# Moving background zero writes into a chain's idle stretches, and selecting row sums ahead of the last chunks

## Chip, cores, metric

One core of one Trainium2 chip. The metric is the device time of one execution in microseconds (us). A run is called slow when it lies more than 1.5% above the fastest run of the same kernel; medians below are of all runs, ratios and their 95% intervals of the fast runs alone.

## The reference

Two layers of attention and MLP for a single token, forward and backward: the output and the gradients of eight inputs.

```python
def _A_ref(x, k_cache, v_cache, wq, wo):          # D 1024, 32 heads of 128, 4 KV heads
    W = min(4096, max(256, Sk // 4))              # Sk 32768, so W = 4096
    q = (x @ wq) ...
    k = jnp.repeat(k_cache[:, :, Sk - W:, :], rep, axis=1)
    v = jnp.repeat(v_cache[:, :, Sk - W:, :], rep, axis=1)
    p = _softmax(einsum(q, k) * Dh ** -0.5)
    return einsum(p, v) ... @ wo
def _B_ref(x, w1, b1, w2):                        # D 1024, F 3584, Mish
    h = x @ w1 + b1
    return (h * jnp.tanh(softplus(h))) @ w2
x = x + _A_ref(_layernorm(x), ...)                # A1
x = x + _B_ref(_layernorm(x), ...)                # B2
x = x + _A_ref(_layernorm(x), ...)                # A3
x = x + _B_ref(_layernorm(x), ...)                # B4
_out, _vjp = jax.vjp(_f, A_x, A_k_cache, A_v_cache, A_wq, A_wo, B_w1, B_b1, B_w2)
```

Only the last 4096 of 32768 rows of the caches are used, so seven eighths of the gradients of both caches are zeros that have to be written: 58.7 MB, a third of all bytes that the kernel moves.

## The kernel before

The zeros are 112 transfers of 0.524 MB from one tile of zeros. A table says how many are issued at which point of the program; `zeros` puts them on the queue of the loads and outputs, `bg_zeros` on GpSimd's queue, behind a small copy that waits for a given tile. What the table leaves goes out at the end (the entry `W2` is read nowhere, so its two zeros do too).

```python
    def zeros(n):
        for _ in range(min(n, len(zero_jobs))):
            nc.sync.dma_start(zero_jobs.pop(0), zt[:])
    def bg_zeros(n, after):
        if n:
            nc.gpsimd.tensor_copy(gate_t[:], after[:, 0:1])
        for _ in range(min(n, len(zero_jobs))):
            nc.gpsimd.dma_start(zero_jobs.pop(0), zt[:])
    ...
    Z = dict(A3=16, B4=[0, 0, 0, 2, 0, 2, 6], A3c=6, A3d=18, W2=2, W1=3, A1c=2, A1d=20, end=8)
```

The chain runs: A1, B2, A3 forward; B4 forward and backward turned into one pass over w1 (below "the MLP", with `B4` the zeros ahead of each of its seven blocks); backward of A3; a second pass over w2; w1 backward; backward of A1; then **the tail**, which makes the weight and cache gradients and stores them. A matrix-vector product by rows streams the weights past the vector and leaves four partial rows in PSUM (the memory that TensorE writes to), from which `rows_sel2` copies and selects the sums as columns:

```python
    def rows_sel2(bank, out_of):
        yr = work.tile([P, 512], FP32, name="yr", tag="kp")
        nc.vector.tensor_copy(yr[:], bank[:])
        for j in range(4):
            mm(out_of(j), yr[:, j * P:(j + 1) * P], sel2[:], out_of.first and j == 0, True)
    ...
        for c in range(NW2):                      # w2_pass, 14 chunks
            w = pre.pop(0) if pre else w2_load(c)
            for tt in range(2):
                rows_y(yrow, w[:, tt, :], a_bf[:, 2 * c + tt:2 * c + tt + 1], tt, c == 0, c == NW2 - 1)
            ...                                   # transposes, ACT copy, DVE reduction, backward columns of c - 1
        bwd1(held.pop(), NW2 - 1)
        rows_sel2(yrow, Cols8(acc.cols(0, TD), False))
        nc.vector.tensor_add(x_new[:], x_col[:], acc.cols(0, TD))
```

Of the kernel before, what the change touches and what calls it, by code (L numbers as in the profile page):

```python
# [23 lines left out]
def kernel(  # L24
# [191 lines left out]
    def acc_tile(n):  # L216
        return pacc.tile([P, n], FP32, name="acc", tag="acc")

    def sm_tile(m, n):
        return pacc.tile([m, n], FP32, name="sm", tag="sm")  # L220
# [9 lines left out]
    def rows_y(bank, row, col, par, start, stop):  # L230

        for half in range(2):
            row_mm(bank, 2 * half + par, col, row[:, half * 512:half * 512 + 512], start, stop)

    def rows_sel2(bank, out_of):

        yr = work.tile([P, 512], FP32, name="yr", tag="kp")
        nc.vector.tensor_copy(yr[:], bank[:])
        for j in range(4):
            mm(out_of(j), yr[:, j * P:(j + 1) * P], sel2[:], out_of.first and j == 0, True)  # L240

# [171 lines left out]
    def attn_fwd(x_col, lname, first):  # L413
# [101 lines left out]
            nc.scalar.activation(p_bf[:, hf * 512:(hf + 1) * 512], hv[hf][:], ACT.Exp, bias=nm2[:, 0:1], scale=1.0)  # L515
        sv["p"] = p_bf
        yrow = acc_tile(512)
        late, early = list(range(NR, NO)), list(range(NR))
        order = early + late if first else late[0:1] + early + late[1:]
        for i, c in enumerate(order):  # L520
            if c not in held and c not in early:
                held[c] = wo_load(c)
            w = wo_kept[c] if c < NR else held.pop(c)
            for tt in range(2):
                rows_y(yrow, w[:, tt, :], o_bf[:, 2 * c + tt:2 * c + tt + 1], tt, i == 0, i == NO - 1)
            if not first and i == 0:
                held[NO - 1] = wo_load(NO - 1)
            if not first:
                if c < NR:
                    xq["wo"].extend(w[:, tt, :] for tt in range(2))  # L530
        yps = sm_tile(P, TD)
        rows_sel2(yrow, Cols8(yps, True))
        x_new = keep.tile([P, TD], FP32, name=f"x_{lname}")
        nc.vector.tensor_add(x_new[:], x_col[:], yps[:])
        return x_new, sv

    def mish_exp(h_ps, n):
# [32 lines left out]
            mm(big[:, t * P:(t + 1) * P], rep8[:, t, :], ident_bf[:], t % 4 == 0, True)  # L570
        return big

    def w2_pass(a_bf, g_bf, x_col, xname, wgname, gbc):

        acc = wide(TD + NW2)
        yrow = sm_tile(P, 512)
        wg = keep.tile([P, NW2, 2], FP32, name=wgname)
        held = []

        def bwd1(w, c):  # L580
            for dch in range(TD):
                mv(acc, TD + c, w[:, 1, dch * P:(dch + 1) * P], g_bf[:, dch:dch + 1], c == 0 and dch == 0, dch == TD - 1)

        for c in range(NW2):
            w = pre.pop(0) if pre else w2_load(c)
            for tt in range(2):
                rows_y(yrow, w[:, tt, :], a_bf[:, 2 * c + tt:2 * c + tt + 1], tt, c == 0, c == NW2 - 1)
            ps = psum1([P, 8, P], BF16, "tps")
            for b in range(TD):
                nc.tensor.transpose(ps[:, b, :], w[:, 1, b * P:(b + 1) * P], ident_bf[:])  # L590
            nc.scalar.copy(w[:, 1, :], ps[:].rearrange("p b c -> p (b c)"))  # L591
            scr = work.tile([P, D], BF16, name="scr", tag="kp")
            nc.vector.tensor_tensor_reduce(out=scr[:], in0=w[:, 0, :], in1=gbc[:], scale=1.0, scalar=0.0,  # L593
                                           op0=ALU.mult, op1=ALU.add, accum_out=wg[:, c, 0:1])
            if held:
                bwd1(held.pop(), c - 1)
            held.append(w)
        bwd1(held.pop(), NW2 - 1)
        rows_sel2(yrow, Cols8(acc.cols(0, TD), False))
        x_new = keep.tile([P, TD], FP32, name=xname)  # L600
        nc.vector.tensor_add(x_new[:], x_col[:], acc.cols(0, TD))
        nc.vector.tensor_copy(wg[:, :, 1:2], acc.cols(TD, TD + NW2)[:, :, None])
        return x_new, wg

    def mlp_fwd(x_col, lname, g_bf):

        n32, n_bf, rstd = ln_fwd(x_col, lname)
        sv = dict(n32=n32, rstd=rstd)
        hacc = wide(TF)
        h_init(hacc.t, 0, TF)  # L610
        for i in range(2 * TD):
            t, hf = i // 2, i % 2
            w = w1_load(i)
            for b in range(NW2):
                fb = hf * NW2 + b
                o = (b // 2) * 2 * P + b % 2
                mv(hacc, fb, w[:, o:o + 2 * P - 1:2], n_bf[:, t:t + 1], False, t == TD - 1)
        a_bf = pair_col("a", lname, TF)
        dact = keep.tile([P, TF], FP32, name=f"dact_{lname}")
        gbc = bcast_row(g_bf)  # L620
        m = mish_exp(hacc.cols(0, TF), TF)
        mish_w(m, hacc.cols(0, TF))
        nc.vector.tensor_mul(a_bf, m["hr"], m["w_"])
        mish_y(m)
        nc.vector.tensor_mul(dact[:], m["y"], m["r"])
        sv["dact"] = dact
        x_new, wg = w2_pass(a_bf, g_bf, x_col, f"x_{lname}", "wg4", gbc)
        return x_new, sv, wg

    CB = 512  # L630
# [8 lines left out]
    def mlp_turn(x_col, lname, wg, g_col, nxt):  # L639
# [28 lines left out]
                xpose(*alt_blocks(wf[:, k * 1024:(k + 1) * 1024], 4), None, True)  # L668

        for b in range(NBK):  # L670
            bg_zeros(Z["B4"][b], dh_bf[:, lo0(b):])
            ws[b] = [w1_block(b, hh) for hh in range(2)]
            lo = b * FB
            sl = slice(lo, lo + FB)
            hps = Wide(pacc.tile([P, FB * R16], FP32, name="sm", tag="sm"), FB)
            h_init(hps.t, lo, FB)
            for t in range(TD):
                for f in range(FB):
                    o = (f // 2) * 2 * P + f % 2
                    mv(hps, f, ws[b][t // HT][:, t % HT, o:o + 2 * P - 1:2], n_bf[:, t:t + 1], False, t == TD - 1)  # L680
            m = mish_exp(hps.cols(0, FB), FB)
            X(b, 0)
            mish_w(m, hps.cols(0, FB))
            q = work.tile([P, HQ], FP32, name="q_", tag="hr2")[:, 0:FB]
            nc.vector.tensor_mul(q, wgf[:, sl], m["r"])
            mish_y(m)
            nc.vector.tensor_mul(dh_bf[:, sl], m["y"], q)
            nc.vector.tensor_mul(dh[:, sl], m["y"], q)
            nc.vector.tensor_mul(a_bf[:, sl], m["hr"], m["w_"])
            ev[0] += 2.4  # L690
            ev[1] += 0.3
            if b:
                M(b - 1)
            X(b, 1)
            fill(4, ["wo", "V", "K", "wq"], None, True)
# [36 lines left out]
    def attn_bwd(g_col, g_bf, lname, sv, first, nxt):  # L732
# [112 lines left out]
            if not first and h % 8 == 7:  # L845
                run(1)
        nps = sm_tile(P, TD)
        rows_sel2(nrow, Cols8(nps, True))
        return ln_bwd(nps[:], sv["n32"], sv["rstd"], g_col, lname, nxt)


# [160 lines left out]
        slots.extend(strm.tile([P, 2048], BF16, name="st_o", tag="st")[:] for _ in range(NB))  # L1012
        dw_tall("w2", TF, out_8.rearrange("(c p t) d -> c p t d", p=P, t=2))

    Z = dict(A3=16, B4=[0, 0, 0, 2, 0, 2, 6], A3c=6, A3d=18, W2=2, W1=3, A1c=2, A1d=20, end=8)


    x1 = None
# [39 lines left out]
    x3, sA3 = attn_fwd(x2, "A3", False)  # L1058
    g3, g3b, sB4 = mlp_turn(x3, "B4", wg4, gcol, "A3")
    g2, g2b = attn_bwd(g3, g3b, "A3", sA3, True, "B2")  # L1060
    x4, wg2 = w2_pass(sB4["a_bf"], g2b, x3, "x_B4", "wg2", bcast_row(g2b))
    dh_of(wg2, "B2", sB2)
    x4_bf = keep.tile([P, TD], BF16, name="x4_bf")
    nc.vector.tensor_copy(x4_bf[:], x4[:])
# [81 lines left out]
```

## Time and profile before

| | before |
|---|---|
| time, median of 2 (range) | 489.98 us (488.81 to 491.14) |
| profiled span | 487.5 us |
| chain, to the start of the last step of A1's backward | 339.9 us |
| from there to the end | 147.6 us |
| zeros issued in the tail | 37 of 112 |

The slices and the table by stretch of this profile stand in the prediction. In the lines of a profile PE is TensorE (matmuls), PEld its weight loads, DVE VectorE, ACT ScalarE, POOL GpSimd and SPq the queue of SyncE; the granted clock is the share of full speed at which TensorE was let run, the DMA share the mean busy share of the 16 DMA engines.

The chain's end is read from the timeline of VectorE (DVE): the start of the instruction that writes the pair gX, the last that every kernel here has before the tail. Span less that time I call "the tail with its lead"; it needs no choice of window and serves to compare all kernels. The stretches of the chain are cut the same way, at the instructions that write x_A (twice), x_B (twice), gA_pair (twice) and gB_pair.

### The profile page before, as it was taken

How to read it: one execution, taken by the hardware profiler on the slowest of the kernel's cores; microseconds unless marked ns; L12 is line 12 of the kernel's file. 1: busy time of each engine (PE TensorE's matmuls, PEld its weight loads, DVE VectorE, ACT ScalarE, POOL GpSimd, SP SyncE). 2: the span in 40 equal slices, each digit the busy share in tenths (PEclk: the TensorE clock that was granted, in tenths of full speed). 3: DMA queues.
4: the chain of work that ended last, by engine and by line, in shares of the span. 5: the costliest groups of instructions: out<-in, count | busy, mean ns of one | idle time of the engine just before them, and what ended most of it. 6: DMA issues, size and time to landing. Idle time of an engine off the chain costs nothing.

```text
span 487.5 us, 11182 instructions
## 1 busy us (share of the span) xinstructions
PE 324.4 (67%) x4700; PEld 213.0 (44%) x4700; DVE 248.6 (51%) x521; ACT 219.5 (45%) x268; POOL 64.1 (13%) x160
## 2 busy tenths in 40 slices
PE   0676654777879998689788877776585873148200
PEld 0344223555549998569467875533311220011000
DVE  2224010573416776535486556455688994169500
ACT  1131100272426887758174536012398995059300
POOL 2000000002400124223001010200821222000000
PEclk9988555595988999998888899556655555555555
DMA  8999988997995799999469998994599999999997
GB/s 326 388 413 413 406 351 319 361 342 283 400 353 183 250 304 404 416 415 414 182 228 366 361 330 314 419 399 179 200 401 408 405 406 403 417 419 415 412 416 308
DMA packets 52253, 172.19 MB, mean 353 GB/s; under 512 B 5200, under 2 KB 12396, under 8 KB 51180
## 3 DMA queue, kind: packets, MB, share of 16 engines
q1 hardware_dynamic: 38816, 123.22, 65.7%
q0 software_dynamic: 13344, 48.25, 25.0%
q8 instruction: 37, 0.61, 0.5%
q14 instruction: 12, 0.10, 0.1%
q10 hardware_dynamic: 44, 0.01, 0.0%
HBM read 72.89 MB, written 98.58 MB: 352 GB/s over the span
## 4 chain that ended last, share of the span: by engine, by line
PE 18%; DMA 16%; issue 7%; DVE 6%; ACT 5%; SPq 1%; POOL 1%; DVEq 0%; ACTq 0%; POOLq 0%
DMA out_dram<-st_o 8%; PE tps L187 6%; DMA w_c<-in_B_w_dram 4%; PE acc L223 3%; DVE wq_b L146 3%; PE ops L223 3%; DMA wo_c<-in_A_wo_dram 2%; DMA out_dram<-so 2%; ACT wo_b L149 2%; PE sm L223 2%; PE d L223 1%; SPq L961 1%; PE tps L590 1%; ACT wo_c L149 1%; DVE st_o L146 1%
## 5 line engine op out<-in xcount | busy, mean ns | idle before, releaser
L139 POOL DMA_DIRECT2D out_dram<-zt x92 | 49.2, 538 | 79.6 <-DMA out_dram<-zt 78.5
L591 ACT COPY w_c<-tps 128x1024 bf16<-128x1024 bf16 x28 | 28.3, 1012 | 24.5 <-PE tps L590 13.8
L146 DVE CAST wo_b<-ops 128x512 bf16<-128x512 f32 (+3 forms) x40 | 33.2, 877 | 9.6 <-PE ops L223 8.1
L593 DVE CUSTOM_DVE_ANT_0 scr<-w_c,gbc 128x1024 bf16<-128x1024 bf16 x28 | 34.2, 1221 | 6.6 <-DMA w_c<-in_B_w_dram 4.5
L149 ACT CAST wo_b<-ops 128x512 bf16<-128x512 f32 (+2 forms) x34 | 27.2, 867 | 17.9 <-PE ops L223 16.5
L149 ACT COPY K<-tps 128x1024 bf16<-128x1024 bf16 x19 | 18.7, 1028 | 28.0 <-PE tps L187 27.9
L223 PEld LDWEIGHTS <-w_c 128*128 128x128 bf16 x672 | 22.9, 101 | 15.6 <-DMA w_c<-in_B_w_dram 10.1
L146 DVE CAST K<-ops 128x1024 bf16<-128x1024 f32 x15 | 17.7, 1222 | 16.0 <-DMA out_dram<-K 15.3
L149 ACT CAST K<-ops 128x1024 bf16<-128x1024 f32 x17 | 16.8, 1013 | 17.7 <-DMA out_dram<-K 15.8
L223 PE MATMUL q<-wq_b,nA_pair 128*32 128x512 bf16 x128 | 13.5, 520 | 16.3 <-DMA wq_b<-in_A_wq_dram 14.8
L149 ACT COPY w_b<-tps 128x1024 bf16<-128x1024 bf16 x20 | 19.5, 1015 | 4.6 <-PE tps L187 4.4
L146 DVE COPY K<-tps 128x1024 bf16<-128x1024 bf16 x13 | 8.8, 689 | 24.9 <-PE tps L187 24.9
L757 DVE CUSTOM_DVE_ANT_0 wo_c<-wo_c,gbc 128x1024 bf16<-128x1024 bf16 x14 | 16.4, 1219 | 9.7 <-DMA wo_c<-in_A_wo_dram 7.6
L187 PE MATMUL tps<-ident_bf,K 128*128 128x128 bf16 x256 | 21.0, 244 | 0.2 <-ACT K L149 0.2
L590 PE MATMUL tps<-ident_bf,w_c 128*128 128x128 bf16 x224 | 20.5, 245 | 0.0
L223 PE MATMUL ops<-Tw 2*128 2x512 bf16 x56 | 15.4, 545 | 5.9 <-ACT wo_b L149 4.1
L187 PEld LDWEIGHTS <-K 128*128 128x128 bf16 x256 | 17.8, 111 | 3.6 <-issue 3.5
L223 PE MATMUL ops<-Two 2*128 2x512 bf16 x64 | 12.5, 597 | 9.9 <-ACT wo_b L149 4.8
L146 DVE CAST st_o<-ops 128x512 bf16<-128x512 f32 (+3 forms) x20 | 16.3, 845 | 5.2 <-DMA out_dram<-st_o 3.7
L590 PEld LDWEIGHTS <-w_c 128*128 128x128 bf16 x224 | 15.1, 109 | 7.9 <-issue 7.9
L187 PE MATMUL tps<-ident_bf,w_c 128*128 128x128 bf16 x224 | 17.2, 237 | 1.9 <-DMA w_c<-in_B_w_dram 1.9
L149 ACT COPY w_c<-tps 128x768 bf16<-128x768 bf16 (+1 forms) x14 | 11.6, 830 | 14.0 <-PE tps L187 12.8
(334 smaller groups left out, 680.5 us busy)
## 6 DMA issues: line engine op xcount, KB each, us to landing
out_dram<-zt POOLq DMA_DIRECT2D x92, 512.0 KB, 12.0
wo_c<-in_A_wo_dram SPq DMA_DIRECT2D x28, 512.0 KB, 6.5
w_c<-in_B_w_dram SPq DMA_DIRECT2D x32, 448.0 KB, 6.0
w_c<-in_B_w_dram SPq DMA_DIRECT2D x28, 512.0 KB, 6.4
out_dram<-zt SPq DMA_DIRECT2D x20, 512.0 KB, 8.6
out_dram<-wo_b SPq DMA_DIRECT2D x18, 512.0 KB, 9.7
wq_b<-in_A_wq_dram SPq DMA_DIRECT2D x16, 512.0 KB, 11.6
out_dram<-K SPq DMA_DIRECT2D x8, 1024.0 KB, 24.5
```

The source lines that it names most:

```text
L139: nc.gpsimd.dma_start(zero_jobs.pop(0), zt[:])
L146: nc.vector.tensor_copy(out_ap, in_ap)
L149: nc.scalar.copy(out_ap, in_ap)
L187: nc.tensor.transpose(ps[:, b, :], ap, ident_bf[:])
L223: nc.tensor.matmul(out_ap, lhsT=lhsT, rhs=rhs, start=start, stop=stop, skip_group_check=True, **kw)
L590: nc.tensor.transpose(ps[:, b, :], w[:, 1, b * P:(b + 1) * P], ident_bf[:])
L591: nc.scalar.copy(w[:, 1, :], ps[:].rearrange("p b c -> p (b c)"))
L593: nc.vector.tensor_tensor_reduce(out=scr[:], in0=w[:, 0, :], in1=gbc[:], scale=1.0, scalar=0.0, op0=ALU.mult, op1=ALU.add, accum_out=wg[:, ...
L757: nc.vector.tensor_tensor_reduce(out=w[:, 0, :], in0=w[:, 0, :], in1=gbc[:], scale=1.0, scalar=0.0, op0=ALU.mult, op1=ALU.add, accum_out=w ...
L961: nc.sync.dma_start(out_v[c], st[:])
```

## The change

Part 1 moves zeros out of the tail into stretches where the DMA row had dips. Part 2 ends the row products early: all but the last two or three chunks go as rows, their sums are copied and selected while the last chunks are awaited, and the last chunks go as column products straight into the same PSUM columns. In the W2 passes VectorE's reduction now writes over the weights in place of a scratch tile, and (not in the cut) the five zeros of the MLP's first block wait for the layer norm's output. The diff cut to its core (the two attentions differ in where the selection stands):

```diff
-    Z = dict(A3=16, B4=[0, 0, 0, 2, 0, 2, 6], A3c=6, A3d=18, W2=2, W1=3, A1c=2, A1d=20, end=8)
+    Z = dict(B2=2, A3=16, B4=[5, 1, 1, 2, 1, 2, 6], A3c=6, A3d=26, W1=3, A1c=4, A1d=28, end=4)
 # attention
+        NRW = NO - 2 if first else NO - 3
-            for tt in range(2):
-                rows_y(yrow, ..., i == 0, i == NO - 1)
+            if i < NRW:
+                for tt in range(2):
+                    rows_y(yrow, ..., i == 0, i == NRW - 1)
+            else:
+                fwd_rows2(yacc, w, c, o_bf, i == NRW, i == NO - 1)
+            if i == NRW - 1:
+                yr = rows_copy(yrow, "v")
+            if i == (NO - 2 if first else NO - 1):
+                rows_sel2(yr, Cols8(yacc.cols(0, TD), False))
 # w2_pass
+            if c < NW2 - 2:
+                rows_y(..., c == 0, c == NW2 - 3)
+            else:
+                fwd_rows2(acc, w, c, a_bf, False, c == NW2 - 1)
-            tensor_tensor_reduce(out=scr[:], in0=w[:, 0, :], ...)
+            tensor_tensor_reduce(out=w[:, 0, :], in0=w[:, 0, :], ...)
+            if c == NW2 - 3:
+                yr = rows_copy(yrow, "a")
+            if c == NW2 - 2:
+                rows_sel2(yr, Cols8(acc.cols(0, TD), False))
         bwd1(held.pop(), NW2 - 1)
-        rows_sel2(yrow, Cols8(acc.cols(0, TD), False))
+        if zn:
+            bg_zeros(zn, wg[:, NW2 - 1, :])
```

More of the change, by code (lines that the diff above doesn't have):

```diff
@@ L233, in rows_y, with rows_copy, rows_sel2 @@
             row_mm(bank, 2 * half + par, col, row[:, half * 512:half * 512 + 512], start, stop)
-    def rows_sel2(bank, out_of):
+    def rows_copy(bank, eng):
         yr = work.tile([P, 512], FP32, name="yr", tag="kp")
-        nc.vector.tensor_copy(yr[:], bank[:])
+        if eng == "v":
+            nc.vector.tensor_copy(yr[:], bank[:])
+        else:
+            nc.scalar.copy(yr[:], bank[:])
+        return yr
+    def rows_sel2(yr, out_of):
         for j in range(4):
@@ L517, in attn_fwd @@
         yrow = acc_tile(512)
+        yacc = Wide(sm_tile(P, TD * R16), TD)
+        NRW = NO - 2 if first else NO - 3
         late, early = list(range(NR, NO)), list(range(NR))
@@ L523, in attn_fwd @@
             w = wo_kept[c] if c < NR else held.pop(c)
-            for tt in range(2):
-                rows_y(yrow, w[:, tt, :], o_bf[:, 2 * c + tt:2 * c + tt + 1], tt, i == 0, i == NO - 1)
+            if i < NRW:
+                for tt in range(2):
+                    rows_y(yrow, w[:, tt, :], o_bf[:, 2 * c + tt:2 * c + tt + 1], tt, i == 0, i == NRW - 1)
+            else:
[4 more added lines that the diff above has]
+                rows_sel2(yr, Cols8(yacc.cols(0, TD), False))
             if not first and i == 0:
@@ L530, in attn_fwd @@
                     xq["wo"].extend(w[:, tt, :] for tt in range(2))
-        yps = sm_tile(P, TD)
-        rows_sel2(yrow, Cols8(yps, True))
         x_new = keep.tile([P, TD], FP32, name=f"x_{lname}")
-        nc.vector.tensor_add(x_new[:], x_col[:], yps[:])
+        nc.vector.tensor_add(x_new[:], x_col[:], yacc.cols(0, TD))
         return x_new, sv
@@ L571, in bcast_row, with w2_pass @@
         return big
-    def w2_pass(a_bf, g_bf, x_col, xname, wgname, gbc):
+    def w2_pass(a_bf, g_bf, x_col, xname, wgname, gbc, zn):
         acc = wide(TD + NW2)
@@ L585, in w2_pass @@
             w = pre.pop(0) if pre else w2_load(c)
-            for tt in range(2):
-                rows_y(yrow, w[:, tt, :], a_bf[:, 2 * c + tt:2 * c + tt + 1], tt, c == 0, c == NW2 - 1)
+            if c < NW2 - 2:
+                for tt in range(2):
+                    rows_y(yrow, w[:, tt, :], a_bf[:, 2 * c + tt:2 * c + tt + 1], tt, c == 0, c == NW2 - 3)
+            else:
+                fwd_rows2(acc, w, c, a_bf, False, c == NW2 - 1)
             ps = psum1([P, 8, P], BF16, "tps")
@@ L591, in w2_pass @@
             nc.scalar.copy(w[:, 1, :], ps[:].rearrange("p b c -> p (b c)"))
-            scr = work.tile([P, D], BF16, name="scr", tag="kp")
-            nc.vector.tensor_tensor_reduce(out=scr[:], in0=w[:, 0, :], in1=gbc[:], scale=1.0, scalar=0.0,
+            nc.vector.tensor_tensor_reduce(out=w[:, 0, :], in0=w[:, 0, :], in1=gbc[:], scale=1.0, scalar=0.0,
                                            op0=ALU.mult, op1=ALU.add, accum_out=wg[:, c, 0:1])
@@ L626, in mlp_fwd @@
         sv["dact"] = dact
-        x_new, wg = w2_pass(a_bf, g_bf, x_col, f"x_{lname}", "wg4", gbc)
+        x_new, wg = w2_pass(a_bf, g_bf, x_col, f"x_{lname}", "wg4", gbc, Z["B2"])
         return x_new, sv, wg
@@ L670, in mlp_turn @@
         for b in range(NBK):
-            bg_zeros(Z["B4"][b], dh_bf[:, lo0(b):])
+            bg_zeros(Z["B4"][b], dh_bf[:, lo0(b):] if b else n_bf)
             ws[b] = [w1_block(b, hh) for hh in range(2)]
@@ L847, in attn_bwd @@
         nps = sm_tile(P, TD)
-        rows_sel2(nrow, Cols8(nps, True))
+        rows_sel2(rows_copy(nrow, "v"), Cols8(nps, True))
         return ln_bwd(nps[:], sv["n32"], sv["rstd"], g_col, lname, nxt)
@@ L1060 @@
     g2, g2b = attn_bwd(g3, g3b, "A3", sA3, True, "B2")
-    x4, wg2 = w2_pass(sB4["a_bf"], g2b, x3, "x_B4", "wg2", bcast_row(g2b))
+    x4, wg2 = w2_pass(sB4["a_bf"], g2b, x3, "x_B4", "wg2", bcast_row(g2b), 0)
     dh_of(wg2, "B2", sB2)
```

## The prediction

> **What bounds the kernel now.** I read the slices of the page first, then a table of busy times by stretch that I cut at the dips of the DMA row, then the waits of the last stretch, then the timelines around the four places where row sums are selected. The slices show the shape: a long chain with dips of the DMA row, and an end in which DMA is full and TensorE is throttled.
>
> ```profile
> PEclk9988555595988999998888899556655555555555
> DMA  8999988997995799999469998994599999999997
> GB/s 326 388 413 413 406 351 319 361 342 283 400 353 183 250 304 404 416 415 414 182 228 366 361 330 314 419 399 179 200 401 408 405 406 403 417 419 415 412 416 308
> ```
>
> The table by stretch (columns: length, busy us of PE, PEld, DVE, ACT and POOL, granted clock, DMA share, GB/s):
>
> ```profile
> 72.00:120.00 48.00, 31.59 (x538) 24.21 (x541) 22.14 (x50) 15.04 (x18) 1.35 (x4) 0.64 0.87 317
> 141.00:165.00 24.00, 20.56 (x418) 19.34 (x408) 13.41 (x54) 13.80 (x19) 0.00 (x0) 0.93 0.64 204
> 237.00:247.00 10.00, 7.05 (x70) 5.17 (x70) 6.87 (x16) 2.02 (x2) 0.00 (x0) 0.66 0.05 17
> 291.00:298.00 7.00, 5.76 (x92) 3.90 (x92) 5.78 (x10) 2.38 (x3) 1.51 (x3) 0.76 0.84 339
> 327.00:347.00 20.00, 13.74 (x113) 7.68 (x113) 10.49 (x30) 5.73 (x10) 5.13 (x27) 0.62 0.35 143
> 456.00:484.70 28.70, 0.00 (x0) 0.00 (x0) 1.28 (x2) 0.00 (x0) 0.00 (x0) 0.50 1.00 405
> 347.00:484.70 137.70, 66.00 (x369) 15.35 (x368) 81.31 (x91) 78.44 (x90) 19.82 (x43) 0.51 1.02 407
> ```
>
> The reader is to see two things. From 347 to 484.7 us the transfers are the bound: share 1.02, 407 GB/s, while the busiest engine, DVE, works 81 of 137.7 us, and the last 28 us are draining alone. Before that, a dependent chain of matrix-vector products is the bound and DMA idles in five places. The waits of the stretch from 405 to 460 us say the same of the tail: the engines wait for the output buffer K until its transfer has landed.
>
> ```profile
> ACT K L149 <- DMA out_dram<-K: 15.8, 2, 11.2
> DVE K L146 <- DMA out_dram<-K: 15.3, 2, 10.9
> ```
>
> **What the Trainium skill says.** "DMA: Bandwidth & Descriptors", section "Issuing engines are not separate DMA queues": transfers of all queues run on the same 16 engines and interleave, so moving zeros between queues gains nothing; only moving them in time does. The trace agrees: 402 GB/s from 347 to 411 us with two queues, 415 from 426 to 456 with one. Same page, "Where 436 GB/s comes from": 435 GB/s is the fabric's ceiling, about 358 what HBM grants a core. Here the trace differs from the second figure: 405 to 415 GB/s are sustained, so I use 407. Same page, "Queues, rings and completion order": an engine takes turns between its queues by packets. So a zero that meets a load slows it; no line of the trace before isolates this. "TensorE: Matmul & The Clock Gate", section "What's actually happening": the array runs at half clock after an idle window. The trace agrees: the eight selecting matmuls take 1.85 us near 114 and 68 us at clock 0.50, but 1.02 us near 146 us at 1.00.
>
> **Part 1, the zeros.** Each zero writes 0.524 MB. At 407 GB/s that is 1.29 us. By the counts in the diff, the tail held 8 + 29 = 37 of the 112 zeros before, and holds 4 + 5 = 9 after: 28 leave it. They go 2 behind the first W2 pass, 8 into the second MLP, 8 behind the first attention-backward loads, 2 and 8 into the last attention backward. (The title says thirty; 2 of the old table were never issued.)
> What leaves the tail: 28 x 0.524 = 14.7 MB. The tail moved 137.7 us x 407 GB/s = 56.0 MB; 41.4 MB stay, 101.6 us. That is 36.1 us less, if DMA stays the bound.
> Does it? From the timelines of the tail the engines' own pace is: 8 chunks of dW2 in about 14 us, 16 of dW1 in 19, 8 of dV in 10, 16 of dWo in 18 with the two row layouts, 8 of dK in 10, 16 of dWq in 16, where I chose the stretches without a DMA wait. Together some 87 us, under 101.6. The nine zeros stand first and give the queue a start of 11.6 us, but dW1 makes 0.459 MB in 1.2 us, as fast as it drains (1.13 us), and dV and dK send only after four chunks. I allow **1.5 us** for an empty queue at such a place.
> What the new places have to offer (length x (1 - share)): behind the first W2 pass (114 to 120 us; shares 0.74 and 0.36 in 3 us slices) 2.7 us for 2.6 us of zeros; 141 to 165 us 8.6, and 1.2 in the 24 us after it, for 10.3; 237 to 247 us 9.5 for 10.3; 291 to 298 us 1.1 for 2.6; 327 to 347 us 13.0 for 10.3. So the zeros fit to within 0.5 + 0.8 + 1.5 = 2.8 us. In the MLP PE is busy all of 150 to 189 us and loads are three blocks ahead, so nothing waits there. After 237 us the extra zeros drain until about 247 us, while the loads whose landing the chain awaits are issued from 245.7 us: I put 0.7 us on the path. After 291 us the seventh load of wo, issued at 297.7 and awaited 4.9 us, may meet the tail of the two extra zeros: 0.7 us. Together **+1.4 us**. The eight after 298 us stand ahead of the output chunks of dW2 on their queue, but those have 17 buffers and no reader, so nothing waits.
>
> **Part 2, row sums earlier.** Before, each of the four passes ended: last row product, DVE copy of the sums, eight selecting matmuls, addition.
>
> ```profile
> 67.24 0.69 DVE L238 COPY yr<-acc 128x512 f32<-128x512 f32 x1 [15.69 <-PE acc L223]
> 69.95 0.16 DVE L534 TENSOR_TENSOR x_A<-x,sm 128x8 f32<-128x8 f32 x1 [2.02 <-PE sm L223]
> 144.90 0.69 DVE L238 COPY yr<-acc 128x512 f32<-128x512 f32 x1 [7.07 <-PE acc L223]
> 146.80 0.16 DVE L534 TENSOR_TENSOR x_A<-x_B,sm 128x8 f32<-128x8 f32 x1 [1.21 <-PE sm L223]
> ```
>
> After, the copy lies beside the last chunks, which go as 16 column products each. From the passes that have such products I take eight to start every 0.28 us in all at full clock and 0.34 at half, so 16 cost 0.56 or 0.68, against 0.35 or 0.55 for the four row products.
> First attention, half clock: the last two chunks land at 65.28 and 66.57 (start of their row products). Columns of chunk 14 to 66.0, selection to 67.9, columns of chunk 15 to 68.6, addition at 68.75 in place of 69.95: **-1.2 us**.
> Second attention, full clock: the last chunk is awaited until 144.45; columns to 145.05, selection (placed after it) to 146.1: **-0.65 us**.
> The two W2 passes: the selection now stands before the last chunk on PE, and that chunk was not awaited (no DMA wait at 111.2 or 260.66 us). Counting on from 109.74 at half clock: columns 0.6, transposes 0.8, backward columns 0.35, selection 1.85, columns 0.7, transposes 0.85, the ACT copy 1.0, backward columns 0.35: addition at 116.5, before 116.07. The second one, from 259.39 at full clock, gives 264.4, before 264.16. So **+0.4 and +0.25 us**: the PE work only changes its place, and column products are dearer. The DVE reduction now overwrites the weights and so waits for PE's rows, but PE has read them by then or sets the pace itself (a chunk each 1.17 to 1.7 us against DVE's 1.27): 0.
> Sum of part 2: **-1.2 us**.
>
> **Sum.** -36.1 + 1.5 + 1.4 - 1.2 = -34.4 us. From the median, 489.98 - 34.4 = 455.6; I say **455.5 us**, 7% less.
>
> **Rivals.** (a) The moved zeros push the loads. The two queues share the engines, and 20 of the 28 zeros go where loads follow. If each held up the chain by its whole 1.29 us, 25.8 us come back: about 481 us. For it: the chain awaits loads at 247 and 255 us (5.6 and 5.2 us). Against it: these stretches were measured idle, at 17 GB/s in the largest. A third of this rival (8 us) would make 463.
> (b) The tail becomes bound by the engines. For it: PE stands at clock 0.50 and DVE and ACT are busy nine tenths of 362 to 411 us, so the margin over 87 us is 15 us of 100. Against it: the drain of 28 us shows how far the engines run ahead. A loss of 3 to 7 us: 458 to 462.
> (c) The zeros were hidden and something else ends the run: 488 us. The share of 1.02 up to the end speaks against it.
> (d) The earlier start of everything and a row sum that vanishes from the path wholly, with no contention: 452 us.
>
> **Range and chances.** The transfer term alone can be off by its rate (402 to 415 GB/s: 35.4 to 36.5 us). Low end: no starved queue, no contention, rate low: 451. High end: a third of (a), or most of (b): 462. Faster by over 2% (under 480.2) fails only if (a) holds almost whole: 0.97, within 0.02, slower 0.01.
>
> **What would show it.** Right: the DMA row is full from about 298 us to the end but for a few us; the stretch from the first zero of the end to the last output is 101 to 104 us, at 400 to 415 GB/s; the DMA share of 237 to 247 us rises from 0.05 to near 1, that of 327 to 347 us from 0.35 to over 0.8; the waits for K's transfer shrink from 15 us to a few; the chain reaches the first chunk of the end within 2 us of where it did (348 us). In part 2: the first attention's sum some 1.2 us earlier, the W2 passes not shorter. Wrong: a longer wait for w_c or wo_c (rival a), or dips in the DMA share of the last 100 us (rival b). A tail of 102 us after a later start would mean that (a) is the size I missed.

## The result, and the profile after

| | before | after |
|---|---|---|
| time, median of 2 (range) | 489.98 us (488.81 to 491.14) | 458.71 us (456.73 to 460.68) |
| ratio of the fast runs | | 0.9362 [0.9164, 0.956] |
| profiled span | 487.5 us | 458.9 us |
| chain | 339.9 us | 346.5 us |
| tail with its lead | 147.6 us | 112.4 us |

A ratio is the mean time of one kernel's fast runs over that of the other's of the same rounds, so not quite the ratio of the medians quoted. The saving of the medians is 31.3 us; 34.5 were predicted. The tail gave 35.2 us, the chain took 6.6 back (in this profile, which is the slower of the two executions). By stretches the two profiles differ by -2.0 us in the first attention, +0.1 from there to the second attention's sum, +2.3 in the MLP, +3.0 in A3's backward, +5.1 in the second W2 pass with w1's backward, and -1.9 in A1's backward: most of what was lost lies behind the MLP. One sign that the prediction named failed here: the tail was to be reached within 2 us of where it was before, and it came 6.6 us later.

The slices of the page after: granted clock, DMA share and rate over the span.

```profile
PEclk9989555596787999996897959878566555555555
DMA  8999999988999999999997879989999999999997
GB/s 322 388 412 413 407 407 355 406 287 309 395 414 355 354 336 332 397 412 417 416 414 285 341 260 347 354 289 413 417 417 377 407 409 403 411 413 403 420 412 284
```

The dips that the row had before are filled but for some tenths. The table by stretch, cut at the same events as the one of before, which come some 5 us later from A3's backward on (columns: length, busy us of PE, PEld, DVE, ACT and POOL, granted clock, DMA share, GB/s):

```profile
141.00:165.00 24.00, 21.31 (x416) 21.25 (x417) 13.37 (x55) 14.77 (x20) 4.74 (x12) 0.86 0.99 347
241.50:251.50 10.00, 7.37 (x82) 5.07 (x82) 6.38 (x15) 3.13 (x4) 0.00 (x0) 0.66 0.73 285
...
332.00:352.50 20.50, 14.18 (x115) 7.08 (x108) 10.47 (x28) 5.41 (x9) 3.98 (x23) 0.59 1.03 418
...
352.50:456.00 103.50, 67.97 (x382) 16.51 (x381) 82.25 (x95) 78.77 (x90) 6.08 (x20) 0.51 1.01 403
```

The share rose from 0.64 to 0.99 in the first half of the MLP, from 0.05 to 0.73 at the end of A3's backward (near 1 was named) and from 0.35 to 1.03 ahead of the tail, and the tail of 103.5 us still runs at a share of 1.01 and 403 GB/s. The waits for K's transfer are gone; these are the two groups of the page that had them (after the bar: idle time just before them, and what ended most of it):

```profile
L146 DVE CAST K<-ops 128x1024 bf16<-128x1024 f32 x15 | 17.8, 1223 | 0.9 <-PE ops L223 0.6
L149 ACT CAST K<-ops 128x1024 bf16<-128x1024 f32 x17 | 17.0, 1012 | 2.0 <-PE ops L223 1.7
```

Part 2, from the timelines of TensorE (PE) and VectorE after: the first attention, then the second (start us, us, engine, line, operation; in brackets the idle time before and what ended it).

```profile
65.21 0.60 PE L223 MATMUL sm<-o_pair,wo_c 128*128 128x16 bf16 x16 [0.67 <-DMA wo_c<-in_A_wo_dram]
65.66 1.85 PE L223 MATMUL sm<-sel,yr 128*128 128x2 f32 x8
67.36 0.57 PE L223 MATMUL sm<-o_pair,wo_c 128*128 128x16 bf16 x16
...
67.98 0.16 DVE L548 TENSOR_TENSOR x_A<-x,sm 128x8 f32<-128x8 f32 x1 [2.70 <-PE sm L223]
...
143.07 0.56 PE L223 MATMUL sm<-o_pair,wo_c 128*128 128x16 bf16 x16 [3.45 <-DMA wo_c<-in_A_wo_dram]
143.49 1.41 PE L223 MATMUL sm<-sel,yr 128*128 128x2 f32 x8
...
144.94 0.16 DVE L548 TENSOR_TENSOR x_A<-x_B,sm 128x8 f32<-128x8 f32 x1 [5.45 <-PE sm L223]
```

The first sum comes at 67.98 in place of 69.95 us. In the second attention 1.87 us pass from the last chunk's landing to the addition, against 2.35 before; but that chunk was awaited for 3.45 us, against 1.93.

### The profile page after: what moved, and what is told of

Same layout as the page of the kernel before. It is cut to its first block, busy times and chain, and to the rows that moved or that the text cites. A ratio compares the mean times of both kernels' runs of the same rounds, so it can differ in the third digit from the quotient of the medians.

```text
span 458.9 us, 11424 instructions
## 1 busy us (share of the span) xinstructions
PE 330.4 (72%) x4808; PEld 219.8 (48%) x4808; DVE 246.9 (54%) x519; ACT 220.4 (48%) x270; POOL 60.8 (13%) x157
## 4 chain that ended last, share of the span: by engine, by line
PE 22%; DMA 10%; issue 8%; ACT 7%; DVE 7%; POOL 1%; DVEq 0%; ACTq 0%; SPq 0%; POOLq 0%
PE tps L187 6%; PE ops L223 5%; DMA w_c<-in_B_w_dram 4%; PE acc L223 4%; DVE wq_b L146 3%; ACT wo_b L149 3%; DMA wo_c<-in_A_wo_dram 2%; PE sm L223 2%; ACT st_o L149 2%; DVE K L146 2%; DMA out_dram<-wo_b 2%; PE d L223 2%; PE tps L607 1%; DMA out_dram<-K 1%; PE rw L895 1%
## 5 line engine op out<-in xcount | busy, mean ns | idle before, releaser
L139 POOL DMA_DIRECT2D out_dram<-zt x84 | 44.9, 538 | 41.5 <-DMA out_dram<-zt 38.5
L609 DVE CUSTOM_DVE_ANT_0 w_c<-w_c,gbc 128x1024 bf16<-128x1024 bf16 x28 | 33.8, 1221 | 13.2 <-PE sm L223 7.6
L223 PEld LDWEIGHTS <-w_c 128*128 128x128 bf16 x736 | 26.1, 103 | 14.7 <-DMA w_c<-in_B_w_dram 9.1
L607 PE MATMUL tps<-ident_bf,w_c 128*128 128x128 bf16 x224 | 21.3, 251 | 0.0
L187 PE MATMUL tps<-ident_bf,w_c 128*128 128x128 bf16 x224 | 18.0, 243 | 2.9 <-DMA w_c<-in_B_w_dram 2.8
L607 PEld LDWEIGHTS <-w_c 128*128 128x128 bf16 x224 | 15.7, 112 | 6.7 <-issue 6.7
L149 ACT COPY w_c<-tps 128x768 bf16<-128x768 bf16 (+1 forms) x14 | 11.6, 830 | 15.0 <-PE tps L187 15.0
L146 DVE COPY w_c<-tps 128x1024 bf16<-128x1024 bf16 (+1 forms) x18 | 11.7, 661 | 12.4 <-PE tps L187 9.0
L149 ACT COPY wq_b<-tps 128x1024 bf16<-128x1024 bf16 x16 | 15.1, 1051 | 4.9 <-PE tps L187 4.9
```

Of the source, the lines that this page charges most:

```text
L146: nc.vector.tensor_copy(out_ap, in_ap)
L149: nc.scalar.copy(out_ap, in_ap)
L187: nc.tensor.transpose(ps[:, b, :], ap, ident_bf[:])
L223: nc.tensor.matmul(out_ap, lhsT=lhsT, rhs=rhs, start=start, stop=stop, skip_group_check=True, **kw)
L607: nc.tensor.transpose(ps[:, b, :], w[:, 1, b * P:(b + 1) * P], ident_bf[:])
L609: nc.vector.tensor_tensor_reduce(out=w[:, 0, :], in0=w[:, 0, :], in1=gbc[:], scale=1.0, scalar=0.0, op0=ALU.mult, op1=ALU.add, accum_out=w ...
```

## The experiments

Three sets of four kernels, each kernel in five rounds, each set on one chip with its own runs of the kernel before: medians of 495.16, 490.53 and 490.83 us. In the first set six of the eleven runs of before are slow, and the record's own verdict on its four kernels is "unclear"; I go by the ratios of the fast runs. One kernel's executions spread: the fast ones of before went from 486.86 us at a mean granted clock of 0.735 to 494.95 at 0.705. So a difference of 2 us between two totals is not resolved, and I read small effects from the stretches of the profiles.

| kernel | zeros in the MLP / the tail | median us (range) | ratio [95%] | MLP | chain | tail with lead |
|---|---|---|---|---|---|---|
| before | 10 / 37 | 489.98 | 1 | 43.8 | 339.9 | 147.6 |
| after | 18 / 9 | 458.71 (456.73 to 460.68) | 0.9362 [0.9164, 0.956] | 46.1 | 346.5 | 112.4 |
| e1 zeros only | 18 / 9 | 459.34 (455.41 to 465.39) | 0.9375 [0.9297, 0.9452] | 47.3 | 341.3 | 112.3 |
| e2 sums only | 10 / 37 | 489.69 (485.91 to 491.43) | 1.0003 [0.9932, 1.0074] | 44.8 | 342.0 | 147.5 |
| e3 MLP's back | 10 / 17 | 468.07 (463.58 to 469.57) | 0.9554 [0.9481, 0.9628] | 44.3 | 344.6 | 122.4 |
| e4 A3's back | 18 / 17 | 468.10 (465.18 to 473.18) | 0.9551 [0.9466, 0.9636] | 44.9 | 343.1 | 122.5 |
| e5 after again | 18 / 9 | 458.54 (456.45 to 461.69) | 0.9347 [0.9298, 0.9395] | 47.3 | 342.6 | 112.8 |
| e6 selection in waits | 18 / 9 | 456.39 (451.22 to 462.86) | 0.9265 [0.9206, 0.9324] | 48.6 | 346.7 | 112.8 |
| e7 none at the end | 18 / 0 | 459.80 (455.84 to 461.55) | 0.9351 [0.9301, 0.9401] | 50.5 | 346.4 | 111.7 |
| e8 warm clock | 18 / 9 | 459.82 (457.44 to 467.13) | 0.9346 [0.9294, 0.9397] | 48.3 | 346.0 | 112.7 |
| e9 more in the MLP | 26 / 1 | 467.61 (465.26 to 475.45) | 0.9507 [0.945, 0.9565] | 56.4 | 354.5 | 112.1 |
| e10 first sum only | 18 / 9 | 456.96 (455.44 to 460.19) | 0.9311 [0.9262, 0.9361] | 46.5 | 341.0 | 112.9 |
| e11 zeros only again | 18 / 9 | 459.70 (457.17 to 468.98) | 0.9348 [0.9296, 0.9399] | 48.5 | 342.7 | 112.5 |
| e12 as e6 | 18 / 9 | 455.98 (453.34 to 457.48) | 0.9277 [0.9223, 0.933] | 46.6 | 343.4 | 112.3 |

The last three columns are of each kernel's profiled execution, in us. That of e6 was in the slow state; its stretches are not used for a verdict. My theory after the result: the tail gave what was reckoned, and the loss is contention in the chain, most of it in the MLP. The rivals: the tail is bound by the engines by now; the loss comes from the sums; or it is the clock.

### e1, e2: each part alone

e1 is the change without part 2 (before's `rows_sel2` and passes); e2 is the change with before's counts of zeros:

```diff
 # e2
-    Z = dict(B2=2, A3=16, B4=[5, 1, 1, 2, 1, 2, 6], A3c=6, A3d=26, W1=3, A1c=4, A1d=28, end=4)
+    Z = dict(B2=0, A3=16, B4=[0, 0, 0, 2, 0, 2, 6], A3c=6, A3d=18, W1=3, A1c=2, A1d=20, end=8)
```

> Only the zeros are moved; the row sums stay as they were. Theory (contention): the tail gives 36 us and the chain before it comes back 5 to 8 us later, because the moved zeros share the engines with loads that the chain awaits; then this kernel takes 459 to 462 us, and its second MLP (from the second attention's sum to the gradient behind it) is near the 45.9 us of the changed kernel, not 43.6 as before. Rival (clock): the chain's loss comes from the throttle's phase, a matter of chance and of the moved selections; then this kernel takes 454 to 457 us and its second MLP 43.6 us.

> Only the row sums are selected earlier; the zeros stay where they were. From the profile of the changed kernel the first attention is 2.0 us shorter and the first W2 pass 0.7 us; on record I had -1.2 us for all four. Theory: 487 to 489 us, 1 to 3 us below before, with the second W2 pass (24.0 us before) within 1 us, since its 26.8 us in the changed kernel come from late loads. Rival: the selection put before the last chunk makes the W2 pass itself longer, 25 us or more, and nothing is won.

The zeros alone gave 0.9375, the sums alone 1.0003. So part 1 is the whole gain that can be seen. In e2 the first attention ended 2.0 us earlier (67.93 us), yet its chain was 342.0 us, 2.1 longer than that of before: the stretch of A3's backward took 54.95 us in place of 49.81. My theory asked for a chain 5 to 8 us longer in e1; it was 1.4 us longer (341.3), less than in e2, which has none of the moved zeros. So the zeros are not the whole of the chain's loss; more on this under e10.

### e3, e4: eight zeros back into the tail, from two places

```diff
 # e3: the MLP's
-    B4=[5, 1, 1, 2, 1, 2, 6]
+    B4=[0, 0, 0, 2, 0, 2, 6]
 # e4: those behind the loads of A3's backward
-    A3d=26
+    A3d=18
```

> The changed kernel with the eight zeros of the second MLP put back to the end. The end grows by 8 x 1.29 = 10.3 us. Theory (contention): the second MLP is back at 43.6 us from 45.9, so the whole is 7.5 to 8 us slower than the changed kernel, 466 to 467 us. Rival (clock): the MLP's length doesn't follow the zeros, the whole is 10 us slower, 469 us.

> The changed kernel with the eight zeros behind the first attention-backward loads put back to the end (18 there as before). The end grows by 10.3 us. Theory (contention): the second W2 pass loses its late loads and is 24.0 to 25 us again, from 26.8, so the whole is 7.5 to 9 us slower than the changed kernel. Rival (clock): the pass stays at 26 to 27 us, since its selection runs at half clock, and the whole is 10 us slower. The attention backward ahead of it (52.8 us, before 49.8) should stay longer under the theory only if zeros matter there, which have not changed before 231 us; so I expect it between 49.8 and 52.8 us by chance of the clock.

Both lengthen the tail with its lead by 10 us (122.4 and 122.5 against 112.3 to 112.9), near the 10.3 us of eight zeros at 1.29. In the whole, e3 and e4 stand at 468.07 and 468.10, some 9 us over e1 of the same set. The MLP of e3 is back at 44.3 us, so its own stretch shows a price of the MLP's eight zeros; that e3 is no faster than e4 in the whole means that this price is not seen in the totals of these runs.

### e5, e7: the change again, and no zeros at the end

e7 leaves out the nine last zeros. It is wrong on purpose: one gradient has unwritten rows.

```diff
 # e7
-    ... end=4)
+    ... end=0)
-    bg_zeros(1000, g0b)
+    del zero_jobs[:]
```

> The changed kernel itself, beside the others on one chip, since its first figure rests on two runs and single executions of one kernel spread by 2%. Contention and clock theory alike: 457 to 461 us, ratio to before near 0.936. If sums and zeros add, its mean lies within 2 us of the zeros-only kernel's.

> The changed kernel without the nine zeros of the end: its result is wrong on purpose, those blocks are not written. It asks what bounds the end. Theory (transfers): 9 x 1.29 = 11.6 us less than the changed kernel, 446 to 449 us, DMA share still 1.0. Rival (engines): the end is bound by PE, DVE and ACT once the zeros are gone, the DMA row shows dips and the gain is under 6 us. From my count of the engines' pace, 87 us, I expect 9 to 11.6 us with a dip or two.

Nine zeros are 11.6 us of transfers, and leaving them out saved nothing: 0.9351 beside 0.9347, tail with its lead 111.7 us beside 112.8. The table by stretch of e7's tail shows why (columns as above):

```profile
354.00:360.00 6.00, 2.79 (x12) 0.50 (x12) 4.59 (x13) 2.91 (x7) 0.06 (x1) 0.63 0.24 100
360.00:366.00 6.00, 5.39 (x18) 1.25 (x18) 4.95 (x9) 5.17 (x11) 0.00 (x0) 0.50 0.83 333
366.00:372.00 6.00, 5.12 (x17) 0.89 (x16) 4.68 (x9) 5.73 (x9) 0.00 (x0) 0.50 0.91 360
372.00:378.00 6.00, 3.22 (x20) 0.80 (x19) 4.48 (x8) 4.54 (x7) 0.00 (x0) 0.50 0.72 288
...
390.00:396.00 6.00, 5.97 (x46) 1.40 (x42) 6.00 (x6) 5.35 (x7) 0.00 (x0) 0.50 0.52 208
...
444.00:450.00 6.00, 0.00 (x0) 0.00 (x0) 0.00 (x0) 0.00 (x0) 0.00 (x0) 0.50 1.02 408
...
354.00:441.00 87.00, 66.96 (x369) 15.73 (x368) 79.22 (x88) 77.78 (x90) 0.06 (x1) 0.51 0.89 357
```

Without zeros the queue is short of work until 396 us: (1 - share) x 6 us of the five rows up to 396 that are below 1 is 4.6 + 1.0 + 0.5 + 1.7 + 2.9 = 10.7 us, about the 11.6 us that the zeros had. Then it is full to the end. So the engines are at work for 87 us (354 to 441), as I had counted, the transfers stay the bound of the last 60 us, and the nine zeros fill places in which nothing else could go. The tail's floor is reached; moving more zeros out of it can win nothing. That is rival (b) of the prediction, true of the next zero and not of the 28 that were moved.

### e9: eight more zeros in the MLP

Since the last zeros cost nothing, moving eight of them into the MLP shows the price there by itself.

```diff
-    B4=[5, 1, 1, 2, 1, 2, 6], ... end=4)
+    B4=[8, 4, 2, 3, 1, 2, 6], ... end=0)
```

> The change with eight of the nine last zeros moved into the second MLP too (26 there in place of 18). A zero at the end costs nothing by the run without them, so this run measures what a zero costs in the MLP by itself. Theory 'zeros there meet the chain': the MLP, 46 to 50 us with 18 zeros and 44.3 with 10, becomes 50 to 56 us, since its transfers are already at a share near 1, and the whole is 4 to 9 us over the change run beside it or in the same state. Rival (my prediction: PE sets the pace there and zeros only fill idle transfers): MLP 46 to 49, whole within 2 us of the change.

The MLP grew to 56.4 us and the whole to 467.61, 9.1 us over the change (458.54 in e5), or 7.9 us by the ratios (0.9507 less 0.9347, of 491 us): eight zeros cost eight or nine tenths of their 10.3 us. The table by stretch over the MLP, of e3 (10 zeros), e5 (18) and e9 (26), one after the other:

```profile
144.41:188.66 44.25, 43.28 (x993) 43.22 (x994) 31.55 (x125) 35.70 (x45) 6.05 (x14) 0.96 0.80 275
```

```profile
142.70:190.00 47.30, 44.36 (x983) 44.02 (x984) 31.57 (x126) 36.19 (x46) 11.04 (x26) 0.94 1.00 358
```

```profile
144.20:200.60 56.40, 46.30 (x993) 45.83 (x994) 31.71 (x125) 35.98 (x45) 15.25 (x34) 0.88 0.99 369
```

And TensorE's waits in the same stretches, of e5 and of e9 (total us, times, longest):

```profile
PE acc L223 <- ACT V L149: 1.4, 1, 1.4
PE sm L223 <- DMA w_b<-in_B_w_dram: 0.7, 1, 0.7
...
```

```profile
PE sm L223 <- DMA w_b<-in_B_w_dram: 9.1, 4, 5.4
...
PE acc L223 <- ACT V L149: 0.4, 1, 0.4
```

With 10 zeros a fifth of the transfer time is idle (0.80) and there is no wait for the weights w_b. With 18 the share is 1.00: full, with 0.7 us of waits. With 26 nearly everything that is added is waited for, 9.1 us; the loads of w_b landed a median of 11.0 us after their issue, against 5.7 in before and 7.5 in e5. The lost clock (0.96 to 0.88) comes with the waits.

Why these loads have so little room is in the timelines. The first three blocks of w1 are issued 10 to 18 us before their first use. From the fourth on a block is issued only when the backward products of the block three before it have begun (158.02 us in before) and its buffers come free, 8.1 us or one and a half blocks before its first use. The fourth block in before, its issue and its first use:

```profile
158.65 0.37 SPq L636 DMA_DIRECT2D w_b<-in_B_w_dram  x1
```

```profile
166.73 0.95 PE L223 MATMUL sm<-nB_pair,w_b 128*128 128x16 bf16 x32
```

In before the five landings of these later blocks that the trace tells took 4.7 to 6.1 us, so 1.9 to 3.4 us were to spare. In e5 the fourth block's second half took 8.8 us and was awaited; in e9 the two halves took 11.4 and 16.9 us, and this is the longest wait:

```profile
173.48 0.60 PE L223 MATMUL sm<-nB_pair,w_b 128*128 128x16 bf16 x16 [5.45 <-DMA w_b<-in_B_w_dram]
```

Over all profiles the MLP takes 43.8, 44.3 and 44.8 us with 10 zeros (mean 44.3) and 44.9 to 50.5 with 18 (the nine profiles in the fast state, mean 47.3): the change pays some 3 us there. What makes it up differs between profiles. Waits for w_b are 0 to 1.5 us, on average 0.4; an ACT copy is awaited for 1.4 us in e5; and what the trace calls "issue" (a wait for nothing that the page shows) is 0 to 3.2 us, on average 1.3: 3.2 at once in e7, 2.1 in four pieces in e1. The rest is not split up; the granted clock of the MLP was 0.96 in the three profiles with 10 zeros and 0.88 to 0.96 in the nine.

The "issue" stops can be told from the DMA packets in the traces. One queue is of the kind "instruction", with 37 packets of 16,384 bytes in each kernel (38 in e8). Over the 14 profiles TensorE has 19 "issue" waits of more than 0.3 us, and every one ended 1.26 to 1.60 us after such a packet had landed: 180.30 and 181.81 us in e7, 163.53 and 164.89 in e1. Of TensorE's other waits of that length 1 to 7% ended so. This speaks for waits for instructions whose transfer came late: 12 of the 19 lie in MLPs with 18 zeros, none in the three MLPs with 10. It isn't a proof: no run varies these transfers, three of the nine MLPs with 18 zeros have no such stop, and neither has e9's.

### e8: matmuls that keep the clock up

e8 adds small idle products ahead of the last chunk of the second attention, in A3's backward and in each layernorm's backward, to test whether half clock there explains the longer chain.

```diff
+    def warm(n):
+        ps = psum1([P, 512], FP32, "wps")
+        for _ in range(n):
+            mm(ps, ident_bf[:], zt[:, 0:512], True, True)
+            if not first and i == NO - 1:          # second attention
+                warm(6)
+            if first and i == len(late) - 1:       # A3's backward
+                warm(6)
+        warm(4)                                    # layernorm's backward
```

> The changed kernel with idle matmuls of zeros (six ahead of the last chunk of wo in the second attention and in the first attention backward, four behind each sum of the layer norm's backward) in stretches in which PE waits. Theory (clock): the rise of the first attention backward from 49.8 to 52.8 us is half clock behind the wait for wo, above all 3.6 in place of 1.9 us for the V products; with PE kept busy it is 49 to 51 us, the V products take 1.9 us and the mean granted clock rises above 0.75; the whole is 2 to 4 us less. Rival: the length comes from loads, the idle matmuls change nothing or delay the path by up to 2 us each, and the whole is the same or 2 us more.

The clock stayed at 1.00 where I had aimed, and the whole did not move (0.9346). A few us later it was lost again, at a stop of 1.86 us among the transposes of wq, again an "issue" stop, some 1.5 us after an instruction packet had landed (221.12):

```profile
222.57 5.62 PE L187 MATMUL tps<-ident_bf,wq_b 128*128 128x128 bf16 x56 [1.86 <-issue]
```

So one place of half clock does not explain the chain.

### e10, e11: the first sum only, and the zeros only again

e10 is e1 with the new form of sum in the first attention alone (its edit is the attention's part of the diff, under `first`); e11 is e1 unchanged.

> The zeros of the change and of the row sums only the first attention's. Theory 'the sums of the W2 passes and of the second attention bring nothing': first attention 68.0 us as in every kernel with it (70 without), whole 1 to 3 us below the zeros alone. The third stretch of interest, the attention backward after the MLP (49.5 to 49.8 us in the two profiles without new sums, 51.8 to 55 in the eight with them): if it is 49 to 50.5 here the new sums of the second attention or W2 lengthen it; if it is 52 to 55, an earlier arrival or chance of the clock does.

> The zeros alone, a second time. Attention backward after the MLP 49.5 us again if the long one belongs to the new sums, 52 to 55 if it is chance. First attention 70.0 to 70.4. Whole within 2 us of the run of the change (458.5), so ratio 0.934 to 0.938.

The first attention takes 67.84 us in e10 and 70.64 in e11, so this gain is sure: 67.8 to 68.3 us in the ten fast profiles with the new first sum, 69.95 to 70.64 in the three without. A3's backward took 49.8, 49.5 and 51.2 us in the profiles with no new sum, 52.5 in e10 and 50.9 to 55.0 in the nine fast ones with all of them. e10 has neither the second attention's new sum nor those of the W2 passes and is long all the same, and e11 is longer than e9. So the new sums there are not shown to lengthen it; an earlier arrival or chance stays open.

Over the longer stretch from the MLP's end to the tail the profiles part more clearly: 149.3, 149.1 and 150.2 us in the three without any new sum, 152.2 in e10, and 152.7 to 156.0 in the nine with all of them, e2 without the moved zeros among them (154.6). TensorE is busy for 118.0 to 118.9 us of it in the first three, 119.7 in e10 and 120.3 to 123.8 in the nine, at a granted clock of 0.81 to 0.83, 0.82, and 0.75 to 0.82. So what the new sums win early is lost behind the MLP, and this loss goes with the sums, not with the zeros. Why is not shown; half clock alone does not do, for e8 had 0.82 there and took 155.0 us. (The profiles of e1 and e11 are each the fastest execution of their kernel, so the gap may be smaller than it looks.)

e10's ratio, 0.9311, is below e11's 0.9348 by less than the intervals are wide.

### e6, e12: the selections inside the waits

In the change the selection of the W2 passes stands ahead of the last chunk, and in the second attention behind it. Here both are moved to where TensorE would wait:

```diff
 # attention
-            if i == (NO - 2 if first else NO - 1):
+            if i == NO - 2:
 # w2_pass
-            if c == NW2 - 2:
+            if c == NW2 - 1:
```

> The changed kernel with the selection moved into waits: in the W2 passes from before the last chunk to behind the last chunk's transposes, where PE waits 0.95 us for the ACT copy; in the second attention from behind the last chunk to before it, where PE waits 3.4 us. Theory of my step: from the start of the last but one chunk's column products to the addition the W2 pass shrinks by 0.9 us, from 6.3 us (107.14 to 113.41 and 264.15 to 270.43 in the changed kernel) to 5.3 or 5.4, and the second attention's sum follows its last chunk's landing by 0.7 us in place of 1.9. Rival: the selection there delays the last backward products and nothing is gained. In the whole it is 0 to -4 us, below what executions of one kernel spread.

> The change with the selections in the waits, a second time, since its first interval overlapped with the change's. If its 0.9265 was real: 1 to 4 us below the zeros alone beside it. The W2 passes 4.0 to 4.4 us from the first column products to the addition (change: 4.8 at full clock, 6.3 at half), the second attention's sum 0.6 us after the last chunk lands (change: 1.5 to 1.9). If it was the state of the chip: within 1 us of the zeros alone.

The second W2 pass of e5, then of e12, both at full clock:

```profile
262.39 0.56 PE L223 MATMUL acc<-a_pair,w_c 128*128 128x16 bf16 x16
...
263.69 1.05 PE L223 MATMUL acc<-sel,yr 128*128 128x2 f32 x8
...
264.60 0.55 PE L223 MATMUL acc<-a_pair,w_c 128*128 128x16 bf16 x16
...
267.18 0.16 DVE L622 TENSOR_TENSOR x_B<-x_A,acc 128x8 f32<-128x8 f32 x1 [0.87 <-PE acc L223]
```

```profile
263.54 0.56 PE L223 MATMUL acc<-a_pair,w_c 128*128 128x16 bf16 x16
...
264.85 0.55 PE L223 MATMUL acc<-a_pair,w_c 128*128 128x16 bf16 x16
...
266.25 1.03 PE L223 MATMUL acc<-sel,yr 128*128 128x2 f32 x8
...
267.54 0.16 DVE L622 TENSOR_TENSOR x_B<-x_A,acc 128x8 f32<-128x8 f32 x1 [0.99 <-PE acc L223]
```

From the first column products to the addition it is 4.8 us in e5 and 4.0 in e12: behind the last chunk's products the selection fits beside ACT's copy of that chunk, which PE awaits anyway (PE stood 0.95 us for it in the first W2 pass of after). In the second attention the time from the last landing to the addition falls from 1.5 us (e5) to 0.6. Two sets gave 0.9265 and 0.9277, against 0.9347 for the change in e5 and 0.9348 for the zeros alone beside e12: 3.5 to 4 us by the ratios, 2.2 and 3.7 by the medians. The intervals just overlap in each set; that both sets agree makes it the likely best version, at 456 us, not a proven one. From e10 of the same set (0.9311) e12 is not told apart.

## Why the prediction was right or wrong

**The tail: right.** Predicted -36.1 + 1.5 = -34.6 us; the tail with its lead fell by 35.2 us, and the stretch from its first zero is 103 us at 403 GB/s, where 101 to 104 at 400 to 415 were named. Adding the eight back costs 10 us (e3, e4), so the 1.29 us a zero hold about as well from 17 zeros to 9. What the prediction did not see is that those nine are free (e7).

**Contention, the term that failed: "In the MLP PE is busy all of 150 to 189 us and loads are three blocks ahead, so nothing waits there."** I set 0; the nine profiles show +3 us. The step that failed is the lead of the loads: three blocks ahead holds for the first three blocks only, from the fourth on it is one and a half, 8.1 us, of which the landings in before left 1.9 to 3.4 us. I summed the idle transfer time and found that the zeros fit to within half a microsecond, but at a share of 1.00 loads landed later (a median of 7.5 us in e5 and 11.0 in e9, 5.7 in before). e9 shows the slope beyond that point, 9 us for 10.3 us of zeros, by waits for w_b. For the 3 us of the change itself only part of the cause is shown: waits for w_b and "issue" stops, 1.7 us together on average. The stops, which go with late instruction packets, were not in my sum at all.

One reading behind it was off too. The 5.6, 5.2 and 4.9 us for which the prediction says that loads are awaited are their times from issue to landing on the critical chain; TensorE itself stood 0.94 us before 252.89, not at all before 260.66, and 1.04 us before 302.66.

**The other two places of contention: not resolved.** I put 0.7 us each on the w2 and the wo loads. The stretch of the second W2 pass took 24.8 us without the extra zeros (e4) and 26.6 and 24.2 with them (after, e5), and that stretch varies more by the clock. A1's backward, with two extra zeros ahead of the wo loads, took 47.4 us in after and 47.3 in e2 without them, so no 0.7 us there. The 2 zeros behind the first W2 pass were counted as free; the last chunk of wo in the second attention was awaited 0.41 us without them (e2), but 1.93 in before, also without, and 1.1 to 3.5 with them. A price of about 1 us is possible and not shown.

**The sums: one term right in kind, the sum not seen.** First attention: -1.2 predicted, -2.0 measured (67.98 against 69.95), because sixteen column products at half clock let the selection start 0.45 us after them, not 0.68, and the selection held up the next chunk for 1.70 us, not 1.9. Second attention: -0.65 predicted; from the landing to the addition -0.5 in after (1.87) and -0.9 in e5 (1.48). W2 passes: +0.4 and +0.25 predicted; from the start of the last but one chunk's forward products to the addition the first takes 6.27 us in after and took 6.33 in before, the second 4.79 in e5 and 4.77 in before, so 0. The local gains add up to some 2.5 to 3 us, but the sums alone gave 1.0003 and the change stands level with the zeros alone (0.9347 and 0.9362 against 0.9348 and 0.9375). By the profiles they are lost again behind the MLP, where every kernel with a new sum took 152.2 us or more and those without 150.2 or less; why stays open, and so does whether part of it only drowns in the spread: 0.9932, the low end of the interval of e2, would still hold the gains.

**The whole.** Predicted -34.4 us, measured -31.3 (two runs each) and -0.065 x 490 = -32 us by e5's ratio. For the chain I had +1.4 - 1.2 = +0.2 us; it took +6.6 in after's profile, +1.4 and +2.8 with the zeros alone (e1, e11) and +2.1 with the sums alone (e2). The 3 us of the MLP would account for the difference in the total, though that price did not show in the total of e3, and more of the chain's loss lies behind the MLP than in it. The rivals: (a) came true in a small form, some 3 us and not 25.8; (b) for the next zero alone; (c) and (d) did not.

## What to carry to other kernels

Background writes moved off a transfer-bound tail paid in full here (28 of them, 35 us) until the tail had empty places of its own; leave just as many as fill the places where the engines have nothing to send, and test it by a run without them. In a chain that also loads, a stretch with idle transfer time takes such writes cheaply but not for nothing: from a share of 0.80 to 1.00 eight writes cost some 3 us here and saved 10 in the tail, beyond it eight more cost 9. Before you count on such a stretch, read from the timeline how long before their use its loads are issued: here buffers that come free late set it. A small serial step such as a selection belongs where its engine waits anyway, which is behind the last load's work in one pass and ahead of it in another (here 0.8 us in a W2 pass and 0.9 in the second attention).

## What the Trainium skill lacked or had wrong

- "DMA: Bandwidth & Descriptors", section "Where 436 GB/s comes from": about 358 GB/s is given as what HBM grants a core, and the prediction took it so. The tails here, which mostly write to HBM, ran at 403 GB/s for 103 us (after), with stretches of 421 (e7). The page is not wrong as a whole: just before it says that this is a core's share when both cores of the memory stream.
- "DMA: Bandwidth & Descriptors", section "Issuing engines are not separate DMA queues": it says that queues share the engines, and the runs agree, but no page says what a background write costs the loads beside it. Here: some 3 us for eight writes of 0.524 MB that raised the share of their stretch from 0.80 to 1.00, 9 us for eight more, with loads that landed after a median of 11.0 us and not 5.7.
- "Runtime: NRT & Kernel Launch", section "Instruction fetch mechanics": it says that instructions are streamed in 16 KiB blocks over a DMA queue of their own, at a cost "mostly hidden". What it costs when the transfers are full no page says. In the MLP TensorE stopped for 3.2 us at once (e7) and 2.1 us in four pieces (e1), at shares of 1.00 and 0.99, and not at all in before, at 0.79; the stops ended 1.26 to 1.55 us after a packet of 16,384 bytes on the instruction queue had landed. That they are waits for such fetches is likely by this, and not proved.
- "TensorE: Matmul & The Clock Gate", section "What's actually happening": it calls the ramp's cost under 1% of a typical span. That speaks of the ramp at a kernel's start; in this chain the clock falls again and again (a mean of 0.718 over the span of before), and the same eight selecting matmuls take 1.05 or 1.87 us in the same place of the same kernel (second W2 pass, e5 and after). What this costs in all no run here shows.
